# Second MLP, first pass two blocks at a time: the read of w_out words moved two groups ahead, sums in a new buffer, streamed pairs of w_in in four transfers

## The chip, the cores and the metric

The kernel runs on one core of one Trainium2 chip. The metric is device time in microseconds. One profiled execution of the kernel before lies beside three timed runs.

## The reference

Attention with a softmax over q's head dimension and over k's sequence, then two MLPs on the 4608 x 512 result, all float32. The part around the change is the second MLP's first product and its activation.

```python
def _moe2_ref(x, w_in, w_out):          # x 4608 x 512, w_in 512 x 2048, w_out 2048 x 512
    h = x @ w_in
    relu6 = np.clip(h + 3.0, 0.0, 6.0)
    g = h * relu6 / 6.0
    return (g @ w_out).astype(np.float32)
```

The weights come in as 64-bit floats, read as pairs of 32-bit words, and the kernel makes float32 of them by integer operations. Each float32 product is made of three matmuls with a high and a low part (`mm3`, L81 to L84).

## The kernel before

Each large product is done by a scheme of seven half-size products instead of eight: operands numbered 1 to 7 are sums and differences of quarters, and the results are added up from seven matmul chains. So a "pair" of w_in, which is 256 of its 2048 columns, is kept as 7 slices of 2 x 128 columns, each with a high and a low part. Such a pair is a tile of 128 x 3584 floats, 1792 KB, and lies ready in DRAM as `wd[1, p]`. There are 8 pairs (NC).

**The first pass of the second MLP** is the loop over `step_in(k)`, 40 steps (L978). Steps 0 to 7 are narrow: one block of 512 tokens, matmuls of 256 columns. Steps 8 to 39 are wide: two blocks at a time, matmuls of 512 columns, four rounds of eight steps (round 0 is steps 8 to 15). Each step uses one pair p = k mod 8 and has 7 products of 6 matmuls, 42 in all. TensorE's order within a step is: product 7 of step k-1, products 6, 2 and 3 of step k, then product 1 of step k+1 (`head`, L903), product 4 of step k-1, product 5 of step k+1 (`head_5`, L917). Behind product 1 stands a ScalarE copy of bank A into bank B (L915, "copy B<-A"), and product 6 needs it. Between the two lie products 4, 5 and 7.

**Streamed pairs.** The odd pairs stay in the core's memory. The even ones share the two buffers of `ring` and are read again each round: when product 4 of an even pair is done, `refill` (L1030) asks for the pair that is used four steps on, in one transfer of 1792 KB on SyncE's queue (`fill`, L291). That is two steps ahead of its first use, product 1 of `head`. Pair 7 is read in the same way after step 2.

**Gates and their stores.** ScalarE makes the relu of each result (L929), VectorE multiplies (L932) into tiles `gh` (two buffers), `gl` (three) and, in narrow steps, `g` (three), and SyncE's queue stores them to DRAM as `gd`: 256 KB for each `gh`, twice a step, 512 KB for `gl`. These transfers stand on the same queue as the pairs.

**Preparation of w_out.** Beside rounds 0 to 2 the kernel turns the second MLP's w_out into operands, pair by pair, and stores them. `weight_jobs` (L1043) writes the jobs of all 8 pairs out as a list of groups, 7 for each pair. `step_in` calls `slot(i)` three times a step (after product 6, after product 3, and at its end), and each call takes one group, but for the five slots in BUSY (L1057). The jobs of a pair, with the tile each uses:

| job | engine | work |
|---|---|---|
| feed | ScalarE's queue | transfer of the next pair's words, 1 MB, into `st` (one buffer) |
| mag | ScalarE | Abs of the words, `st` to `w` (L132); it waits until the words are there |
| floor, shift, sign, low | VectorE | integer operations on `w`; sign and low also read `st` |
| sum_0, sum_1 | GpSimd | four differences and sums of quarters of `w`, written into `st` itself (L196) |
| high_0, low_0, keep_0 | ScalarE, VectorE, ScalarE's queue | first 3 slices of the pair: high part, low part, store of 768 KB |
| high_1, low_1, keep_1 | the same | the other 4 slices, from the sums: high part (L212), low part (L216), store of 1 MB (L223) |

Because the sums lie in `st`, `feed` can be asked for only when low_1 has read them. Its group is the sixth of the seven, two groups ahead of the `mag` that needs the words.

All engines take their instructions in the program's order. The order is fixed by the code, so a waiting instruction holds back all behind it on its engine or queue.

Of the kernel before, what the change touches and what calls it, by code (L numbers as in the profile page):

```python
# [9 lines left out]
F32R = mybir.dt.float32r  # L10
# [7 lines left out]
P = 128  # L18
# [20 lines left out]
def attention_two_mlps(ctx: ExitStack, tc: tile.TileContext, kqT, kv5, qn, w1, w2, out):  # L39
    nc = tc.nc  # L40
# [28 lines left out]
    def f32(ap):  # L69
        return ap.bitcast(F32)  # L70
# [91 lines left out]
    wd = {}  # L162
# [19 lines left out]
    def operands_w(m, p, new_r, new_s, get_w, add=nc.vector):  # L182

        x = {}

        def sums(k):
            w = get_w()
            if k == 0:
                x["s"] = new_s()
            a22, a11, a12, a21 = (w[:, j * 256:(j + 1) * 256] for j in range(4))  # L190
            s1, s2, s3, s4 = (x["s"][:, j * 256:(j + 1) * 256] for j in range(4))
            for o, a, b, op in (
                (s1, a21, a22, ALU.add), (s2, s1, a11, ALU.subtract),
                (s3, a11, a21, ALU.subtract), (s4, a12, s2, ALU.subtract),
            )[2 * k:2 * k + 2]:
                add.tensor_tensor(out=o, in0=a, in1=b, op=op)  # L196

        def parts(k):
            src, n = ((get_w()[:, :768], 3), (x["s"], 4))[k]
            o = slice(0, 3) if k == 0 else slice(3, 7)  # L200
            src = src.rearrange("p (s n) -> p s n", n=256)
            if m == 2:
                return x["r", k][:, 0], x["r", k][:, 1], src
            return x["r"][:, 0, o], x["r"][:, 1, o], src

        def high(k):
            if m == 2:
                x["r", k] = m2_p[0].tile([P, 2, 3 + k, 2 * P], F32R, tag=f"r{k}", name="r")
            elif k == 0:
                x["r"] = new_r()  # L210
            h, l, src = parts(k)
            nc.scalar.copy(h, src)  # L212

        def low(k):
            h, l, src = parts(k)
            nc.vector.tensor_tensor(out=l, in0=src, in1=f32(h), op=ALU.subtract)  # L216

        def store_part(k):
            if (m, p) not in wd:
                wd[m, p] = dram.tile([P, 14 * 256], F32, tag=f"wd{m}{p}", name="wd")  # L220
            d = wd[m, p].rearrange("p (h s n) -> p h s n", h=2, n=256)
            o = slice(3 * k, 3 + 4 * k)
            nc.scalar.dma_start(out=d[:, :, o], in_=f32(x["r", k] if m == 2 else x["r"][:, :, o]))  # L223

        def keep():
            wd[m, p] = d = dram.tile([P, 14 * 256], F32, tag=f"wd{m}{p}", name="wd")
            nc.scalar.dma_start(out=d, in_=f32(x["r"]).rearrange("p h s n -> p (h s n)"))

        if m:
            keep_part = store_part if (m, p) != (1, STAYS) else lambda k: None  # L230
            return [
                (0.85, lambda: sums(0)), (0.85, lambda: sums(1)), (0, lambda: high(0)), (0.95, lambda: low(0)),
                (0, lambda: high(1)), (1.2, lambda: low(1)), (0, lambda: keep_part(0)), (0.5, lambda: keep_part(1)),
            ]
        return [
            (0.85, lambda: sums(0)), (0.85, lambda: sums(1)), (0, lambda: high(0)), (0.95, lambda: low(0)),
            (0.6, lambda: high(1)), (0.6, lambda: low(1)), (0.5, keep),
        ]
# [48 lines left out]
    def load_w(g):  # L287
        m, t, p = place(g)
        fill(ring_tile(g), m, p if g != PER + 1 else 2)

    def fill(r, m, p):  # L291
        nc.sync.dma_start(out=f32(r).rearrange("p h s n -> p (h s n)"), in_=wd[m, p])
# [737 lines left out]
    def refill(k):  # L1030
        p = k % NC
        if p % 2 == 0 and k + 4 < STEPS:
            n = (p + 4) % NC
            second_in[n] = r = ring_tile(2 * PER + k)
            fill(r, 1, n)
        if k == 2:
            fill(second_in[7], 1, 7)
        if k >= STEPS - NC and p in OUT_AFTER:
            load_out(OUT_AFTER.index(p))

    OUT_AFTER = (1, 3, 4, 5, 6, 7)

    def weight_jobs():  # L1043
        jobs, late = [], []
        for p in range(NC):
            c = [c[1] for c in second(p, 1, add=nc.gpsimd)]
            mag, floor, shift, sign, low, sum_0, sum_1, high_0, low_0, high_1, low_1, keep_0, keep_1 = c
            more = [feed] * (p < NC - 1)
            jobs += [
                late + [mag], [floor, shift], [sign], [low, sum_0, sum_1], [high_1], [low_1, keep_1, *more],  # L1050
                [high_0, low_0],
            ]
            late = [keep_0]
        return jobs + [late]

    weights_2 = []
    BUSY = {(0, 0), (6, 2), (7, 0), (7, 1), (7, 2)}  # L1057
# [1 line left out]
    def side_in(k):  # L1059
        b, p = divmod(k - NC, NC)  # L1060
        f = lambda i, *parts: [lambda part=part: form_wide(i, part) for part in parts]
        sm = lambda i: [lambda: sums_wide(i)]
        if b < 0:
            table = {
                (0, 2): [lambda: load_wide(0, 0)], (2, 2): sm(0), (3, 1): sm(1), (3, 2): sm(2), (4, 1): sm(3),
                (4, 2): f(1, 0), (5, 0): f(1, 1) + f(5, 0), (5, 2): f(5, 1), (6, 0): f(6, 0) + [feed],
                (6, 1): f(6, 1), (7, 1): f(2, 0), (7, 2): f(2, 1) + f(3, 0, 1),
            }
        else:
            table = {(0, 0): f(7, 0), (0, 1): f(7, 1), (0, 2): f(4, 0, 1)}  # L1070
            if b < WIDE - 1:
                table.update({
                    (1, 0): [lambda: load_wide(b + 1, 0)], (1, 1): [lambda: load_wide(b + 1, 1)],
                    (3, 0): sm(0), (3, 2): sm(1), (4, 1): sm(2), (5, 0): sm(3),
                    (6, 2): f(1, 0, 1) + f(5, 0), (7, 0): f(5, 1) + f(6, 0), (7, 1): f(6, 1) + f(2, 0),
                    (7, 2): f(2, 1) + f(3, 0, 1),
                })

        def slot(i):
            if 0 <= b < WIDE - 1 and (p, i) not in BUSY and weights_2:  # L1080
                for fn in weights_2.pop(0):
                    fn()
            for fn in table.get((p, i), ()):
                fn()
            if b == WIDE - 1:
                if (p, i) == (0, 0):
                    while weights_2:
                        for fn in weights_2.pop(0):
                            fn()
                    prep.close()  # L1090
                    out_p["a"] = stack("out_a", 1, early, side="right")
                    load_g(0)
                    load_g(1)
                for fn in ahead_of_out().get((p, i), ()):
                    fn()

        return slot
# [240 lines left out]
    with tc.manual_schedule():  # L1338
# [107 lines left out]
        head_5(0)  # L1446
        for k in range(STEPS):
            step_in(k, side_in(k))
        step_in(STEPS, lambda i: None)
        step_out(0, 2)  # L1450
        step_out(1)
# [64 lines left out]
```

## Time and profile before

| what | value |
|---|---|
| median of three runs | 1680.01 us (1678.97 to 1680.22) |
| profiled execution, its own time | 1683.46 us |
| span of the profile | 1681.7 us, mean granted TensorE clock 0.986 |
| TensorE busy | 1616.2 us, 96% of the span |
| VectorE, ScalarE, GpSimd busy | 1182.7, 758.4, 248.3 us |
| moved by DMA | 412 MB, 245 GB/s over the span |

TensorE is busy nearly all the time, so the page's 40 slices matter more than its sums: 39 of TensorE's busy digits are 8 or 9, and the few 8s show where it waited. Time comes back only where TensorE is idle, or where its clock is at the lower of its two levels.

### The profile page before, as it was taken

The numbers are of one execution on the slowest core, as the hardware profiler recorded it, in microseconds if no ns is written. First come the engines' busy times: TensorE is split into PE (matmuls) and PEld (weight loads), VectorE is DVE, ScalarE is ACT, GpSimd is POOL, SyncE is SP. The second block draws the span as 40 slices with busy tenths as digits, with TensorE's granted clock in tenths as the row PEclk, the third lists the DMA queues.
The fourth block names the chain that finished last, engine by engine and source line by source line (L and its number), as shares of the span: only waits on it lengthen the run. The fifth ranks groups of instructions, "written<-read, shape, count | busy, mean of one in ns | idle before, by whom it ended". The sixth has DMA issues, their size and how long they took to land. (4 is left out here: it accounts for less than half of the span.)

```text
span 1681.7 us, 25454 instructions
## 1 busy us (share of the span) xinstructions
PE 1616.2 (96%) x9768; PEld 1397.3 (83%) x9768; DVE 1182.7 (70%) x1834; ACT 758.4 (45%) x1291; POOL 248.3 (15%) x174
## 2 busy tenths in 40 slices
PE   6999999999999999999999899989899999999998
PEld 4455888989898888888889877767678999999998
DVE  5999677575656657567876476657565787777775
ACT  4454555454444545444544445435354343333332
POOL 2121332222122222200000113120400000000000
PEclk8999999999999999999999999989999999999999
DMA  8488768778787878558897877877788943333332
GB/s 281 150 306 302 263 212 290 246 260 265 234 279 232 302 241 277 203 223 329 317 378 288 313 280 256 318 276 271 266 301 288 376 149 126 126 126 126 126 127 75
DMA packets 87330, 412.16 MB, mean 245 GB/s; under 512 B 12840, under 2 KB 16936, under 8 KB 63528
## 3 DMA queue, kind: packets, MB, share of 16 engines
q1 hardware_dynamic: 75048, 351.02, 59.5%
q10 hardware_dynamic: 12160, 59.51, 9.4%
q8 instruction: 77, 1.26, 0.3%
q14 instruction: 45, 0.37, 0.1%
HBM read 311.43 MB, written 99.06 MB: 244 GB/s over the span
## 5 line engine op out<-in xcount | busy, mean ns | idle before, releaser
L1262 PE MATMUL M<-kout,f 128*128 128x256 f32 x2268 | 275.4, 282 | 0.5 <-DVE f L1168 0.5
L1262 PEld LDWEIGHTS M<-kout,f 128*128 128x128 f32 x2268 | 273.4, 189 | 0.9 <-DVE f L1168 0.7
L82 PE MATMUL y<-gs,woh 128*128 128x512 f32 x512 | 204.6, 400 | 0.0
L83 PE MATMUL y<-gs,woh 128*128 128x512 f32 x512 | 202.5, 395 | 0.0
L84 PE MATMUL y<-gs,wol 128*128 128x512 f32 x512 | 200.1, 391 | 0.0
L79 DVE TENSOR_TENSOR gs<-g,gs 128x512 fp32r<-128x512 f32 x128 | 111.9, 875 | 62.7 <-ACT gs L78 62.2
L1166 ACT CAST f<-gt 128x1024 fp32r<-128x1024 f32 x72 | 75.5, 1049 | 178.1 <-PE M L1262 97.0
L681 ACT ACTIVATE g<-A 128x512 f32<-128x512 f32 x72 | 43.1, 598 | 186.9 <-DVE A L841 171.6
L82 PE MATMUL B<-o,ring 128*128 128x256 f32 x408 | 118.3, 290 | 7.9 <-DVE B L846 4.6
L82 PE MATMUL A<-op,ring 128*128 128x256 f32 x408 | 115.9, 284 | 1.7 <-DMA ring<-wd 1.7
L78 ACT CAST gs<-g 128x512 fp32r<-128x512 f32 x128 | 79.2, 618 | 83.0 <-DVE g L683 80.0
L84 PE MATMUL B<-o,ring 128*128 128x256 f32 x408 | 115.5, 283 | 0.0
L83 PE MATMUL B<-o,ring 128*128 128x256 f32 x408 | 115.3, 283 | 0.0
L83 PE MATMUL A<-op,ring 128*128 128x256 f32 x408 | 115.2, 282 | 0.1
L84 PE MATMUL A<-op,ring 128*128 128x256 f32 x408 | 115.2, 282 | 0.0
L84 PEld LDWEIGHTS y<-gs,wol 128*128 128x128 f32 x512 | 96.5, 188 | 21.7
L1168 DVE TENSOR_TENSOR f<-gt,f 128x1024 fp32r<-128x1024 f32 x72 | 88.0, 1222 | 30.6 <-ACT f L1166 29.6
L82 PEld LDWEIGHTS y<-gs,woh 128*128 128x128 f32 x512 | 96.9, 189 | 12.7
L83 PEld LDWEIGHTS y<-gs,woh 128*128 128x128 f32 x512 | 97.2, 190 | 8.7
L82 PEld LDWEIGHTS B<-o,ring 128*128 128x128 f32 x408 | 77.4, 190 | 25.9 <-DVE B L846 8.9
L1262 PE MATMUL M<-ring,f 128*128 128x256 f32 x756 | 93.5, 282 | 0.4 <-DVE f L1168 0.4
L1262 PEld LDWEIGHTS M<-ring,f 128*128 128x128 f32 x756 | 91.6, 191 | 0.7 <-DVE f L1168 0.6
(336 smaller groups left out, 3792.9 us busy)
## 6 DMA issues: line engine op xcount, KB each, us to landing
ring<-wd SPq DMA_DIRECT2D x84, 1792.0 KB
gt<-gd SPq DMA_DIRECT2D x36, 1024.0 KB
st<-w_dram SPq DMA_DIRECT2D x16, 1024.0 KB
st<-w_dram ACTq DMA_DIRECT2D x16, 1024.0 KB
gd<-gh SPq DMA_DIRECT2D x64, 256.0 KB
gd<-gl SPq DMA_DIRECT2D x32, 512.0 KB
ev<-kv_dram SPq DMA_DIRECT2D x24, 640.0 KB
wd<-ring ACTq DMA_DIRECT2D x8, 1792.0 KB
```

The costliest lines, as they stand in the source:

```text
L78: nc.scalar.copy(hi, src)
L79: nc.vector.tensor_tensor(out=lo, in0=src, in1=f32(hi), op=ALU.subtract)
L82: nc.tensor.matmul(o, lhsT=wh, rhs=xh, start=start, stop=False, **kw)
L83: nc.tensor.matmul(o, lhsT=wh, rhs=xl, start=False, stop=False, **kw)
L84: nc.tensor.matmul(o, lhsT=wl, rhs=xh, start=False, stop=stop, **kw)
L681: nc.scalar.activation(out=a, in_=hb, func=AF.Tanh, scale=0.5)
L1166: nc.scalar.copy(o[0], src)
L1168: nc.vector.tensor_tensor(out=o[1], in0=src, in1=f32(o[0]), op=ALU.subtract)
L1262: nc.tensor.matmul(M[:, h * 2 * P:(h + 1) * 2 * P], lhsT=a, rhs=b, start=p == 0 and h == 0 and e == 0, stop=p == NC - 1 and e == 2, skip_g ...
```

## The change

Three parts, all in the second MLP's first pass.

1. The groups of `weight_jobs` are cut anew. `feed` moves from the sixth group to the fourth, directly behind `low`, so the read is asked for four groups ahead of the `mag` that needs it. high_0 and low_0 come before high_1 and low_1 and each stands in a group of its own; keep_0 comes one group behind low_0, high_1 three groups behind the sums, low_1 one group behind high_1, keep_1 one group behind low_1. A pair's last two groups are merged with the next pair's first two. The list has 58 groups, one more than before, for 57 slots: the last group, keep_1 of the last pair, is issued at the first slot of round 3.
2. The sums are written into the low half of the tile `r1` (tag "r1"), where low_1 later puts its result, and no longer into `st`.
3. A streamed pair is read in four transfers (high and low part, slices 0 to 3 and 4 to 6: 512, 384, 512, 384 KB). `refill` only notes them; each slot issues one (two in narrow steps). Pair 7 is asked for after step 3 instead of step 2.

```diff
         def sums(k):
             w = get_w()
-            if k == 0:
+            if k == 0 and m == 2:
+                x["r", 1] = m2_p[0].tile([P, 2, 4, 2 * P], F32R, tag="r1", name="r")
+                x["s"] = f32(x["r", 1][:, 1]).rearrange("p s n -> p (s n)")
+            elif k == 0:
                 x["s"] = new_s()
...
         def high(k):
-            if m == 2:
-                x["r", k] = m2_p[0].tile([P, 2, 3 + k, 2 * P], F32R, tag=f"r{k}", name="r")
+            if m == 2 and k == 0:
+                x["r", k] = m2_p[0].tile([P, 2, 3, 2 * P], F32R, tag="r0", name="r")
+            elif m == 2:
+                pass
...
+    pieces = []
+
+    def fill_in_pieces(r, p):
+        d = wd[1, p].rearrange("p (h s n) -> p h s n", h=2, n=2 * P)
+        for h in range(2):
+            for a, b in ((0, 4), (4, 7)):
+                pieces.append((f32(r[:, h, a:b]), d[:, h, a:b]))
+
+    def next_piece():
+        if pieces:
+            o, i = pieces.pop(0)
+            nc.sync.dma_start(out=o, in_=i)
...
         if p % 2 == 0 and k + 4 < STEPS:
             n = (p + 4) % NC
             second_in[n] = r = ring_tile(2 * PER + k)
-            fill(r, 1, n)
-        if k == 2:
-            fill(second_in[7], 1, 7)
+            fill_in_pieces(r, n)
+        if k == 3:
+            fill_in_pieces(second_in[7], 7)
...
             jobs += [
-                late + [mag], [floor, shift], [sign], [low, sum_0, sum_1], [high_1], [low_1, keep_1, *more],
-                [high_0, low_0],
+                late + [mag], last + [floor, shift], [sign], [low, *more, sum_0, sum_1], [high_0], [low_0],
+                [keep_0, high_1],
             ]
-            late = [keep_0]
-        return jobs + [late]
+            late, last = [low_1], [keep_1]
+        return jobs + [late, last]
...
             for fn in table.get((p, i), ()):
                 fn()
+            for _ in range(2 if b < 0 else 1):
+                next_piece()
...
         for k in range(STEPS):
             step_in(k, side_in(k))
+        while pieces:
+            next_piece()
```

How the instructions now stand, at three places. **ScalarE, round 1**, from the cast of a pair's second part (before) and from the read of the next pair's words (now) to the Abs that needs those words (L132) and the copy B<-A behind it. `st` is the tile of words, `d_8737` holds `w`, `r` the operands, `wd` their home in DRAM. Before:

```order
L915 COPY B_10089<-A_10088 128x512
L929 ACTIVATE gh<-A_10076,half 128x512
L926 COPY s_10112<-C_10105 128x512
L929 ACTIVATE gl<-B_9931,half 128x512
L223 DMA wd<-r 256x1x1024
L106 DMA st<-w_dram 128x2048
L929 ACTIVATE gh<-d_8737,half 128x512
L212 CAST r<-d_8737 128x768
L929 ACTIVATE gl<-A_10088,half 128x512
L223 DMA wd<-r 256x1x768
L132 ACTIVATE d_8737<-st 128x1024
L915 COPY B_10169<-A_10168 128x512
```

and now:

```order
L106 DMA st<-w_dram 128x2048
L947 ACTIVATE gl<-A_10038,half 128x512
L217 CAST r<-d_8737 128x768
L933 COPY B_10121<-A_10120 128x512
L947 ACTIVATE gh<-A_10107,half 128x512
L944 COPY s_10144<-C_10137 128x512
L947 ACTIVATE gl<-B_9956,half 128x512
L947 ACTIVATE gh<-d_8737,half 128x512
L228 DMA wd<-r 256x1x768
L217 CAST r<-r 128x1024
L947 ACTIVATE gl<-A_10120,half 128x512
L132 ACTIVATE d_8737<-st 128x1024
```

Between the read and its Abs stood three computing instructions; now there are nine, and no store of 1 MB stands directly ahead of the read.

**SyncE's queue, narrow steps.** `ring` and `k_8733` are pairs being read (`k_8733` is pair 7), `gd` the stores of gates. Before:

```order
L292 DMA ring<-wd 128x3584
L951 DMA gd_8871<-g_8806 128x1024
L951 DMA gd_8871<-g_8868 128x1024
L292 DMA ring<-wd 128x3584
L292 DMA k_8733<-wd 128x3584
L951 DMA gd_8998<-g_8929 128x1024
```

and now:

```order
L969 DMA gd_8870<-g_8806 128x1024
L307 DMA ring<-wd 128x1024
L307 DMA ring<-wd 128x768
L307 DMA ring<-wd 128x1024
L307 DMA ring<-wd 128x768
L969 DMA gd_8870<-g_8867 128x1024
L969 DMA gd_8999<-g_8932 128x1024
L307 DMA ring<-wd 128x1024
L307 DMA ring<-wd 128x768
L307 DMA ring<-wd 128x1024
L307 DMA ring<-wd 128x768
L969 DMA gd_8999<-g_8996 128x1024
```

A pair now stands behind the store of its step instead of ahead of it, and the two pairs that stood back to back are parted by a store.

**SyncE's queue, wide steps**, one streamed pair and the stores up to the next. Before:

```order
L292 DMA ring<-wd 128x3584
L973 DMA gd_9330<-gh 128x512
L975 DMA gd_9298<-gl 128x1024
L973 DMA gd_9330<-gh 128x512
L973 DMA gd_9492<-gh 128x512
L975 DMA gd_9298<-gl 128x1024
L973 DMA gd_9492<-gh 128x512
L292 DMA ring<-wd 128x3584
```

and now:

```order
L307 DMA ring<-wd 128x1024
L307 DMA ring<-wd 128x768
L991 DMA gd_9345<-gh 128x512
L307 DMA ring<-wd 128x1024
L991 DMA gd_9508<-gh 128x512
L993 DMA gd_9312<-gl 128x1024
L307 DMA ring<-wd 128x768
L991 DMA gd_9508<-gh 128x512 x2
L993 DMA gd_9475<-gl 128x1024
L307 DMA ring<-wd 128x1024
```

No store of a gate stands behind more than two pieces, and a pair's last piece is issued a step after its first.

## Rows read from the trace of the kernel before

**Rows 1.** Busy time by window; columns: window, length, engines' busy us (instructions), clock, DMA share, GB/s.

```profile
950.00:970.00 20.00, 15.71 (x80) 14.05 (x80) 11.71 (x18) 8.38 (x13) 0.00 (x0) 0.83 0.76 294
1010.00:1030.00 20.00, 16.03 (x59) 12.33 (x58) 11.67 (x17) 8.86 (x13) 11.35 (x7) 0.83 0.85 307
1090.00:1110.00 20.00, 12.09 (x42) 9.30 (x41) 10.48 (x15) 6.83 (x12) 0.00 (x0) 0.74 0.82 287
1190.00:1210.00 20.00, 16.03 (x60) 12.94 (x61) 12.15 (x18) 8.97 (x14) 5.12 (x2) 0.83 0.76 291
```

**Rows 2.** Who TensorE waited for, 930 to 1260 us; columns: total us, times, longest us.

```profile
PE B L82 <- ACT B L915: 19.7, 7, 7.9
PE B L82 <- DVE B L981: 3.5, 1, 3.5
PE A L83 <- DVE fw L594: 2.5, 4, 0.8
PE B L82 <- DVE d L981: 2.3, 2, 1.1
PE A L82 <- DMA ring<-wd: 1.7, 1, 1.7
PE A L82 <- DVE gh L932: 1.6, 1, 1.6
```

**Rows 3.** Timeline of TensorE; columns: start us, us, instruction, [idle before <- releaser].

```profile
934.01 0.39 PE L82 MATMUL A<-op,ring 128*128 128x256 f32 x1 [1.67 <-DMA ring<-wd]
953.52 0.58 PE L82 MATMUL B<-o,k 128*128 128x256 f32 x1 [3.49 <-DVE B L981]
...
1019.02 0.79 PE L82 MATMUL B<-e,k 128*128 128x512 f32 x1 [3.97 <-ACT B L915]
...
1101.00 0.79 PE L82 MATMUL B<-e,ring 128*128 128x512 f32 x1 [7.91 <-ACT B L915]
...
1193.97 0.80 PE L82 MATMUL B<-e,ring 128*128 128x512 f32 x1 [5.45 <-ACT B L915]
```

**Rows 4.** Timeline of ScalarE and its queue (ACTq) before the two longest waits.

```profile
1088.62 0.66 ACTq L106 DMA_DIRECT2D st<-w_dram  x1
...
1099.34 1.12 ACT L132 ACTIVATE d<-st 128x1024 f32<-128x1024 f32 x1 [7.92 <-DMA st<-w_dram]
...
1187.07 1.05 ACT L212 CAST r<-st 128x1024 fp32r<-128x1024 f32 x1 [2.30 <-POOL st L196]
...
1190.64 0.52 ACTq L223 DMA_DIRECT2D wd<-r  x1
1191.19 2.11 ACTq L106 DMA_DIRECT2D st<-w_dram  x1
1193.34 0.57 ACT L915 COPY B<-A 128x512 f32<-128x512 f32 x1 [4.64 <-issue]
```

**Rows 5.** Timeline of SyncE's queue in the narrow steps: two pairs asked for.

```profile
923.85 0.32 SPq L292 DMA_DIRECT2D ring<-wd  x1
...
936.09 0.43 SPq L292 DMA_DIRECT2D k<-wd  x1
```

**Rows 6.** Timeline of VectorE in the narrow steps: a gate waits for its buffer.

```profile
950.70 0.69 DVE L932 SCALAR_TENSOR_TENSOR g<-a,A 128x512 f32<-128x512 f32 x1 [5.45 <-DMA gd<-g]
```

**Rows 7.** Who ScalarE waited for, 930 to 1260 us: the relu of gh.

```profile
ACT gh L929 <- DMA gd<-gh: 21.7, 9, 4.9
```

**Rows 8.** Busy time by window, as rows 1: first MLP, narrow steps, round 1, round 3.

```profile
841.00:884.00 43.00, 42.78 (x266) 38.07 (x265) 33.02 (x52) 18.61 (x31) 2.39 (x1) 1.00 0.97 380
914.00:965.00 51.00, 45.84 (x347) 44.77 (x346) 22.06 (x41) 19.98 (x38) 7.17 (x3) 0.93 0.82 309
1048.00:1140.60 92.60, 81.86 (x338) 64.38 (x337) 61.02 (x79) 42.17 (x63) 16.56 (x12) 0.94 0.79 287
1216.00:1300.00 84.00, 83.86 (x362) 67.58 (x362) 54.49 (x78) 42.32 (x64) 0.00 (x0) 1.00 0.85 301
```

**Rows 9.** Groups by line, 914 to 1320 us: VectorE's job low (x8).

```profile
L150 DVE SCALAR_TENSOR_TENSOR d<-st,d 128x1024 uint32<-128x1024 uint32 x8 | 9.7, 1218 | 0.0
```

More of the change, by code (lines that the diff above doesn't have):

```diff
@@ L1043, in weight_jobs @@
     def weight_jobs():
-        jobs, late = [], []
+        jobs, late, last = [], [], []
         for p in range(NC):
```

## Prediction

> **What bounds the kernel now.** The first view is busy time by window. In round 3, from 1216 to 1300 us, TensorE works 83.86 of 84 us at the full clock [rows 8], 362 matmuls in all, so a wide step of 42 takes 42 x 84 / 362 = 9.75 us, and there is nothing to gain there. The windows of [rows 1] look different: TensorE is idle for 4 to 8 of their 20 us, and the granted clock is 0.74 to 0.83, a mixture of the full 2.4 GHz and of 1.2 GHz. All four lie between 950 and 1210 us, beside the narrow steps and rounds 0 to 2.
>
> The second view says whom TensorE waited for. Its six rows add up to 31.3 us, and 19.7 of them are waits of product 6 for ScalarE's copy of bank A into bank B [rows 2]. The timeline then gives each long gap its time: 3.49, 3.97, 7.91 and 5.45 us [rows 3], one in each of the four windows. So the clock fell beside the four gaps of 3.49 to 7.91 us, and not after that of 1.67. What the lower clock takes is (1 - clock) times 20 us: 3.4, 3.4, 5.2 and 3.4 us [rows 1], 15.4 us together. Gaps and clock make 31.3 + 15.4 = 46.7 us. That is all that this stretch can give back.
>
> The third view is the engine that TensorE waited for. At 1099 us ScalarE's Abs stood 7.92 us for the words of the next pair, 10.7 us after their read had been issued at 1088.62, and the copy stood behind it [rows 4]. At 1190 us it was a chain: the cast of the sums waited 2.30 us for GpSimd, VectorE's low part waited for that cast, and the store and the read, which stand ahead of the copy on ScalarE's queue, waited for VectorE, so the copy was 4.64 us late [rows 4]. The gap of 3.49 us has another root: VectorE waited 5.45 us for a gate buffer whose store had not landed [rows 6], because two pairs stood ahead of it on SyncE's queue.
>
> **The change part by part.**
>
> *The groups of the jobs.* A slot is 9.75 / 3 = 3.25 us. The read of words goes from two groups ahead of the Abs (6.5 us) to four (13 us). It took at most 10.7 us in the row above, and there a store of 1 MB stood directly ahead of it, so the Abs finds its words. The cast of the sums now comes three groups after them, and each low part and store a group behind what it needs, so the chain is gone too. I take off all waits for the copy, 19.7 us, and the clock of their three windows, 3.4 + 5.2 + 3.4 = 12.0: **minus 31.7 us**.
>
> What is new there: the read must wait until VectorE's `low` has read `st`, and this time it stands in the same group. `low` takes 1.22 us [rows 9]; with a gate's multiply ahead of it (0.69 us, as in [rows 6]) and 0.66 us to issue [rows 4], ScalarE is held up to 2.6 us. The copy behind it has products 4, 5 and 7 as cover, 18 matmuls of 9.75 / 42 us, 4.2 us, and takes 0.57. So it costs nothing; if ScalarE comes late to it, it costs about 1 us at each of the slots that stand just ahead of a copy, three of the seven, which the range holds. The sums on GpSimd now wait for the store of `r1`, issued two groups (6.5 us) before; they are wanted three groups later, 9.75 us, and GpSimd is otherwise idle: nothing.
>
> *Pieces, narrow steps.* The gaps of 1.67 and 3.49 us and the clock of their window, 3.4, are 8.6 us. The store of a gate now stands behind one pair at most, so the 3.49 should shrink. But these steps are short of transfers: 309 GB/s for 51 us is 15.8 MB [rows 8], and without the 8.6 us it would be 15.8 / 42.4 = 372 GB/s, as much as the fullest stretch of the trace, 380 GB/s. Pair 7 is asked for a step later than before (it was at 936.09 [rows 5]), and every pair behind a store. Bounds: all 8.6 us back, or 3 us worse, about one further gap like the 3.49. I take half: **minus 4.3 us**.
>
> *Pieces, wide steps.* The relu of gh waited 21.7 us in nine places for its buffer's store [rows 7]. ScalarE's waits show on TensorE as the rows "d" and "gh" of [rows 2], 2.3 + 1.6 = 3.9 us. With stores between pieces I take half back: **minus 2.0 us**. The 2.5 us for "fw" are the operands of the next two blocks; the change does not touch them, and they stay.
>
> The last piece of a pair is issued three slots after the first and used three slots, 9.75 us, after that. A whole pair of 1792 KB, issued at 923.85 [rows 5], was there at 934.01 [rows 3], 10.2 us, behind whatever stood ahead of it. A piece of 512 KB should take a third, so no piece is late: nothing, with the rival below for the other end.
>
> *New costs.* The last store of w_out falls into the first slot of round 3, and one of two loads for the second pass waits on SyncE's queue until it has landed, with stores and two pieces behind: **plus 1 us** (0 to 3.4). And rounds 0 to 2 get tighter. Round 1 moved 287 GB/s for 92.6 us, 26.6 MB [rows 8]; in 8 x 9.75 = 78 us that is 341 GB/s, nine tenths of 380. Short waits come back: **plus 3 us** (0 to 12).
>
> Sum: -31.7 - 4.3 - 2.0 + 1 + 3 = **-34.0 us**. The profiled execution took 1683.46 us (span 1681.7 and 1.8 around it) and would take 1649.5. The median of the runs is 1680.01, 3.4 us below it, so I predict **1646 us**.
>
> **The rivals.**
>
> *Transfers become the bound.* Round 3 ran at 301 GB/s with the DMA engines 0.85 busy and no wait [rows 8]. If rounds 0 to 2 can't move more than that, 26.6 MB take 88.4 us, and each of two rounds like round 1 gives 4 us, the narrow steps 4: about 1668 us. For it: the queues are 0.79 busy already and the pieces add 57 transfers. Against it: 380 GB/s for 43 us at 0.97 [rows 8], with loads and stores mixed. The Trainium skill, page "DMA: Bandwidth & Descriptors", section Specifications, puts the share of HBM of one core at about 358 GB/s. The first row of [rows 8] is above that, so the measurement decides; by the page 341 would be 95% of the limit, and this rival likelier than I make it.
>
> *The read is asked sooner and is late all the same*, because ScalarE gets to it late (it waits for VectorE) or one buffer of words is not free. Then the Abs keeps its long wait, 7.91 + 5.2 us, and the time is about 1659. Against it: the order shows nine instructions between them now, and the only readers of `st` left are sign and low.
>
> *Slower: the queue pays for every piece.* If SyncE's queue dealt with its transfers one after the other, each with a fixed cost, the five transfers of a step (three stores, two pieces) would not fit into 9.75 us, and TensorE would stand at product 1 or 6 of each streamed pair. There are 14 pairs whose load starts in a wide step. Late by 3.5 us each, without any loss of clock, they cost 49 us: 1695 us. It decides from 34 / 14 = 2.4 us on. Against it: round 3 already has 3.5 transfers a step with 2.0 MB, and SyncE's pairs left no gap in TensorE there. The Trainium skill has this cost, on the same page, section "Anatomy of one DMA": about 2.0 us for each and the bytes at 436 GB/s. One after the other, that would be an estimated 11.5 us for a step before and 14.5 us now, 28 x 4.75 = 133 us more than the 9.75. But round 3's step of 9.75 us is already less than 11.5 [rows 8], so by the trace the fixed part of one transfer passes beside others, and I give this little.
>
> *No change*: the waits move to another place of the same length. Half the 46.7 us would have to come back as new gaps and clock; I see no single place for it.
>
> **How the numbers follow.** The forecast has 0.62, the transfers 0.15, the late read 0.13, slower 0.07, no change 0.03. A difference of 0.2%, 3.4 us, is about what a measurement of this kernel can tell from none. Faster is 0.62 + 0.15 + 0.13 = 0.90, same 0.03, slower 0.07. The forecast's own range is 1638 (all of the 8.6 us back, nothing new) to 1655 (12 us of short waits). Eight in ten reach to the two rivals on the same side: 1638 to 1668.
>
> **What would show it.** The waits of TensorE for "ACT B" fall from 19.7 us to under 3; the Abs (L132) has no wait for `st`; the cast of `r` none for GpSimd; the clock is 1.00 in every 20 us window from 970 to the end of the pass; round 1 takes 78 to 82 us at 330 GB/s; what is left lies in the narrow steps, at "ring", "k" or "g". I am wrong if a new row of TensorE's waits names a DMA of `ring` in wide steps, if the clock still falls there, or if round 1 stays near 90 us.

## The result and the profile after

The changed kernel takes 1661.45 us, the median of four runs (1656.24 to 1667.13), against 1679.49 for the kernel before (1677.62 to 1680.22): a ratio of 0.9895, 95% interval 0.986 to 0.993. It is faster, by 18 us where 34 were forecast. The profiled execution of the changed kernel is the shortest of its four, 1656.24 us with a span of 1654.4 and a mean clock of 0.995.

First the question on which most of the forecast rested: whom does TensorE wait for now? The view of waits, 930 to 1260 us; columns as in [rows 2]:

```profile
PE A L84 <- DMA ring<-wd: 12.4, 6, 5.3
PE A L82 <- DMA ring<-wd: 1.0, 1, 1.0
PE A L84 <- DMA k<-wd: 0.8, 1, 0.8
PE A L83 <- DVE fw L612: 0.8, 1, 0.8
PE B L84 <- DMA ring<-wd: 0.3, 1, 0.3
```

The seven waits for ScalarE's copy, 19.7 us in [rows 2], have no row left. Those for VectorE's "B", "d" and "gh" are gone too. In their place stands a row that was not there: pieces of streamed pairs, 12.4 us in six waits, all at L84, the matmul that takes the low part. Busy time by window, the four windows of [rows 1] and then rounds 1 and 2:

```profile
950.00:970.00 20.00, 16.69 (x96) 13.98 (x95) 10.50 (x16) 9.80 (x15) 0.00 (x0) 1.00 0.74 277
1010.00:1030.00 20.00, 20.00 (x88) 16.20 (x87) 15.06 (x20) 10.54 (x17) 6.96 (x6) 1.00 0.96 353
1090.00:1110.00 20.00, 20.00 (x88) 16.19 (x87) 16.50 (x20) 11.12 (x17) 6.06 (x3) 1.00 0.87 316
1190.00:1210.00 20.00, 19.86 (x86) 15.79 (x85) 15.76 (x21) 12.98 (x19) 0.00 (x0) 1.00 0.72 251
...
1036.60:1116.40 79.80, 78.48 (x337) 62.97 (x336) 63.97 (x81) 43.49 (x64) 15.86 (x12) 1.00 0.89 319
1116.40:1196.50 80.10, 78.86 (x338) 62.83 (x338) 61.40 (x79) 43.45 (x64) 20.40 (x16) 1.00 0.85 305
```

The granted clock is 1.00 in all four windows where it was 0.74 to 0.83, and TensorE fills three of them. Round 1 takes 79.8 us, not 92.6 [rows 8], at 319 GB/s. Where the new waits lie, by the timeline of TensorE:

```profile
930.61 0.39 PE L84 MATMUL A<-op,ring 128*128 128x256 f32 x1 [1.49 <-DMA ring<-wd]
942.98 0.39 PE L84 MATMUL A<-op,ring 128*128 128x256 f32 x1 [2.15 <-DMA ring<-wd]
949.05 0.38 PE L84 MATMUL A<-op,k 128*128 128x256 f32 x1 [0.80 <-DMA k<-wd]
955.06 0.50 PE L82 MATMUL A<-fw,ring 128*128 128x512 f32 x1 [1.02 <-DMA ring<-wd]
957.28 0.50 PE L84 MATMUL A<-fw,ring 128*128 128x512 f32 x1 [1.49 <-DMA ring<-wd]
...
1075.05 0.51 PE L84 MATMUL A<-fw,ring 128*128 128x512 f32 x1 [1.18 <-DMA ring<-wd]
...
1154.57 0.50 PE L84 MATMUL A<-fw,ring 128*128 128x512 f32 x1 [0.82 <-DMA ring<-wd]
...
1219.53 0.80 PE L84 MATMUL A<-fw,ring 128*128 128x512 f32 x1 [5.27 <-DMA ring<-wd]
```

Five lie in the stretch that is called narrow below (the last two at product 1 of step 8, the first wide one). Three more, of 1.18, 0.82 and 0.28 us, lie in rounds 1 and 2. The longest, 5.27 us, is at the start of round 3, where the kernel before had no wait. What stands behind it is read from ScalarE's queue (ACTq), from SyncE's, and from the waits of SyncE's queue:

```profile
1202.96 0.52 ACTq L228 DMA_DIRECT2D wd<-r  x1
...
1201.79 0.44 SPq L1149 DMA_DIRECT2D gt<-gd  x1
1211.70 0.32 SPq L1149 DMA_DIRECT2D gt<-gd  x1
1212.11 0.38 SPq L991 DMA_DIRECT2D gd<-gh  x1
1212.55 0.42 SPq L307 DMA_DIRECT2D ring<-wd  x1
...
1214.75 0.43 SPq L307 DMA_DIRECT2D ring<-wd  x1
```

```profile
SPq L1149 <- DMA wd<-r: 9.4, 1, 9.4
```

At 1202.96 ScalarE's queue issues the last store of w_out, the 58th group. SyncE's queue stands before the second load for the second pass (L1149) until 1211.70, and the view of waits gives that row 9.4 us, "DMA wd<-r". Behind it stand the stores of gates and the last two pieces of a pair, its low part, at 1212.55 and 1214.75. TensorE wants the first of the two at 1214.26 (1219.53 less 5.27) and goes on at 1219.53. The clock pays too; the window behind the gap:

```profile
1220.00:1224.00 4.00, 4.00 (x11) 3.03 (x11) 1.31 (x3) 1.18 (x2) 0.00 (x0) 0.50 0.57 220
```

**Stage by stage.** The first matmul of product 5 marks each step in TensorE's timeline. From step 3's to step 8's is called "narrow" here, from 8's to 16's round 0, then rounds 1 and 2, and from 32's to 37's the start of round 3. An undisturbed round is 78 us (8 x 9.75), the start of round 3 is 49.2. One profiled execution each, us; medians and ratios (to the kernel before on the same chip, 95%) are of the timed runs:

| kernel | narrow | round 0 | round 1 | round 2 | start of 3 | median | ratio |
|---|---|---|---|---|---|---|---|
| before | 33.99 | 85.32 | 92.57 | 91.71 | 49.16 | 1679.49 | 1 |
| changed | 33.82 | 77.61 | 79.80 | 80.05 | 57.36 | 1661.45 | 0.9895 (0.986 to 0.993) |
| changed, again | 37.93 | 78.91 | 79.53 | 79.69 | 56.80 | 1660.69 | 0.9897 (0.988 to 0.9913) |
| whole pairs | 34.70 | 78.97 | 79.78 | 80.45 | 51.45 | 1653.15 | 0.9856 (0.9837 to 0.9875) |
| pieces alone | 34.51 | 84.69 | 91.09 | 88.06 | 49.24 | 1679.1 | 1.001 (0.9993 to 1.0027) |
| store early | 34.29 | 77.60 | 79.33 | 79.67 | 49.16 | 1649.35 | 0.984 (0.9824 to 0.9856) |
| store early, whole pairs | 32.48 | 78.73 | 80.34 | 80.45 | 49.16 | 1651.78 | 0.9839 (0.9821 to 0.9858) |
| store early, whole in narrow | 34.25 | 77.85 | 79.84 | 80.22 | 49.17 | 1648.56 | 0.9827 (0.98 to 0.9853) |
| pair 7 sooner | 36.10 | 79.85 | 79.33 | 79.29 | 49.21 | 1647.69 | 0.9816 (0.9796 to 0.9837) |
| read late | 35.09 | 79.61 | 79.97 | 84.90 | 49.16 | 1654.09 | 0.9853 (0.9831 to 0.9876) |
| old grouping | 36.55 | 79.76 | 80.64 | 83.38 | 49.18 | 1657.12 | 0.986 (0.9838 to 0.9883) |
| pair 7 first | 39.14 | 78.93 | 79.46 | 80.43 | 49.22 | 1657.19 | 0.9857 (0.9835 to 0.988) |
| high pieces at once | 31.77 | 78.02 | 79.78 | 79.41 | 49.19 | 1645.63 | 0.9801 (0.9784 to 0.9819) |
| four pieces at once | 32.49 | 77.98 | 80.23 | 80.27 | 49.19 | 1648.39 | 0.9818 (0.9801 to 0.9834) |

From "store early" on, every row has the last store of w_out within round 2 ("old grouping" by its own list).

### The profile page after: what moved, and what is told of

It reads as the page before. It is cut to its first block, busy times and chain, and to the rows that moved or that the text cites. A ratio compares the mean times of both kernels' runs of the same rounds, so it can differ in the third digit from the quotient of the medians.

```text
span 1654.4 us, 25538 instructions
## 1 busy us (share of the span) xinstructions
PE 1603.8 (97%) x9768; PEld 1389.2 (84%) x9768; DVE 1191.4 (72%) x1834; ACT 758.5 (46%) x1291; POOL 247.3 (15%) x174
## 4 chain that ended last, share of the span: by engine, by line
PE 66%; DVE 8%; DMA 7%; ACT 2%; issue 2%; SPq 0%; ACTq 0%; DVEq 0%
PE M L1282 19%; PE y L82 6%; PE y L83 5%; PE y L84 5%; PE A L84 4%; PE B L82 4%; PE A L83 4%; PE B L84 4%; PE A L82 4%; PE B L83 4%; DMA ring<-wd 4%; DMA gd<-gh 2%; DMA gt<-gd 2%; PE C L84 1%; PE C L83 1%
## 5 line engine op out<-in xcount | busy, mean ns | idle before, releaser
L84 PE MATMUL y<-gs,wol 128*128 128x512 f32 x512 | 200.2, 391 | 0.0
L84 PE MATMUL A<-op,ring 128*128 128x256 f32 x408 | 115.4, 283 | 3.6 <-DMA ring<-wd 3.6
L84 PE MATMUL B<-o,ring 128*128 128x256 f32 x408 | 115.2, 282 | 0.0
L84 PEld LDWEIGHTS y<-gs,wol 128*128 128x128 f32 x512 | 96.4, 188 | 21.7
```

What stands on the lines that cost most here:

```text
L84: nc.tensor.matmul(o, lhsT=wl, rhs=xh, start=False, stop=stop, **kw)
```

## The experiments

### The changed kernel again

No edit.

> The changed kernel once more, for its spread and a second profile. It ran between 1656 and 1667 us where the kernel before stays within 3 us. Theory A (two places are marginal: a streamed pair is waited for in the narrow steps and at the start of round 3, and each gap sometimes brings the lower clock with it): median 1656 to 1667, and the profile has its gaps at just these two places, 12 to 22 us in all, rounds 0 to 2 within 2 us of 8 x 9.75 = 78 each. Theory B (rounds 0 to 2 are at the limit of transfers and run differently each time): gaps in the wide steps of rounds 0 to 2 too, a round of over 82 us.

It measured 1660.69 us in five runs (1658.26 to 1666.96), so the 1661 us hold. The rounds and the start of round 3 agree with the first profile within 1.3 us; the narrow steps do not, 37.93 against 33.82. Busy time by window, 908 to 965 us, first of the changed kernel, then of this run:

```profile
908.00:965.00 57.00, 49.25 (x369) 46.18 (x368) 26.74 (x47) 22.71 (x41) 7.16 (x3) 1.00 0.79 293
```

```profile
908.00:965.00 57.00, 50.06 (x351) 47.77 (x350) 24.46 (x45) 19.78 (x38) 7.17 (x3) 0.90 0.78 290
```

TensorE is busy longer and does less: 351 matmuls against 369, at a clock of 0.90 against 1.00. The gaps differ by less than 1 us each (1.49, 2.15, 0.80, 1.02 and 1.49 above; 1.77, 1.85, none at pair 7, 1.86 and 1.46 here), and the clock falls in one execution and not in the other.

### Which part does it: the groups with whole pairs, the pieces alone

"Whole pairs": the changed kernel with streamed pairs read in one transfer, pair 7 after step 2.

```diff
-            fill_in_pieces(r, n)
-        if k == 3:
-            fill_in_pieces(second_in[7], 7)
+            fill(r, 1, n)
+        if k == 2:
+            fill(second_in[7], 1, 7)
```

> The new groups and the new home of the sums, with whole pairs in one transfer, as before. Theory A (the groups carry the gain, 32 us by the prediction's term, the last store costs 7.5 us of it, the pieces give next to nothing): 1650 to 1660 us, no wait of TensorE for the copy B<-A. Theory B (the pieces carry a good part, because stores of gates stood behind whole pairs): 1665 us or more, with waits for gate buffers back in rounds 1 and 2.

"Pieces alone": the kernel before with the pieces, their functions and their calls in the slots, and nothing else of the change.

```diff
-            fill(r, 1, n)
-        if k == 2:
-            fill(second_in[7], 1, 7)
+            fill_in_pieces(r, n)
+        if k == 3:
+            fill_in_pieces(second_in[7], 7)
```

> The pieces alone, with the groups and the sums' home of the kernel before. Theory A: the four long waits for the copy stay, 1675 to 1685 us, no change to be measured or a little slower in the narrow steps. Theory B: 1660 to 1670 us.

TensorE's waits, 930 to 1260 us, of the pieces alone and then of the whole pairs with the new groups:

```profile
PE B L82 <- ACT B L928: 12.9, 6, 5.7
PE A L84 <- DMA ring<-wd: 9.6, 7, 2.1
```

```profile
PE B L82 <- DVE B L999: 3.8, 1, 3.8
PE B L82 <- DVE d L999: 3.1, 3, 1.1
PE B L82 <- ACT B L933: 2.0, 1, 2.0
```

The pieces alone leave the waits for the copy (L928 is its line there), add waits for pieces, and change the time by nothing that twelve runs can tell: 1.001 (0.9993 to 1.0027). The groups and the sums' home (the two were not parted) do all of it: with whole pairs the kernel is faster than the change as made, 1653.15 us. So the change's own pieces cost it 7.5 us (1660.69 less 1653.15), and the table says where: the start of round 3 is 51.45 us with whole pairs and 57.36 with pieces. SyncE's queue waits for the last store as long (11.3 us there), but a whole pair had been asked for at 1198.30, ahead of the wait; with pieces two of its four stood behind it. What the late store still costs with whole pairs, 51.45 against 49.16 us, is one wait of TensorE for the copy, 2.04 us: the copy stands behind a relu that waits 9.14 us for its gate's buffer.

### The last store a group sooner

```diff
-        return jobs + [late, last]
+        return jobs + [late + last]
```

> The changed kernel with the last store of w_out in the last group of round 2, one group earlier than the first slot of round 3, so that there are 57 groups. Theory A (SyncE's queue stood 9.4 us because a load for the second pass waited for this store, and the pair's third piece behind it came late): the wait of SyncE's queue for the store is gone, the gap of 5.3 us at the third piece in round 3 and the low clock behind it too, 7.5 us less than the changed kernel, about 1654. Theory B (two loads of 1 MB ahead of the pieces are what makes them late): the gap stays at 3 us or more, and the time within 3 us of the changed kernel.

> New groups and sums' home, the last store in round 2, whole pairs in one transfer: against the run with the last store early it takes away the pieces alone. Theory A (with the store out of the way the pieces neither cost nor bring anything): within 2.5 us of that run, 1647 to 1652. Theory B (pieces let stores of gates through in wide steps): 1652 us or more, with TensorE waits for gates in rounds 0 and 1. Theory C (each piece costs something on the queue): 1646 or less.

The second is the same with whole pairs. "Store early" measured 1649.35 us (1647.51 to 1654.74), 11 less than the changed kernel on the same chip. SyncE's queue has no wait for "wd<-r" any more, and the start of round 3 is 49.16 us as in the kernel before. That place is 7.6 to 8.2 of the 11 us. The other 3 can't be placed: the narrow steps, whose code is the same in both, take 34.29 us here and took 33.82 and 37.93 in the two profiles of the changed kernel. Its waits of TensorE:

```profile
PE A L84 <- DMA ring<-wd: 5.4, 5, 1.7
PE A L84 <- DMA k<-wd: 2.4, 1, 2.4
PE A L83 <- DVE fw L612: 0.8, 1, 0.8
```

With whole pairs it is 1651.78, ratios 0.9839 and 0.984: once the store is out of the way, the pieces are neither a gain nor a loss that these runs can tell. They do what the prediction took them for at the gates, though. The relu's wait for its buffer, 930 to 1260 us, with the store early in both, first with whole pairs and then with pieces, and last with the pieces alone in the old groups:

```profile
ACT gh L947 <- DMA gd<-gh: 45.9, 17, 6.6
```

```profile
ACT gh L947 <- DMA gd<-gh: 23.9, 10, 4.5
```

```profile
ACT gh L942 <- DMA gd<-gh: 9.9, 5, 3.9
```

In the old groups the pieces bring the 21.7 us of [rows 7] down to 9.9. In the new groups the shorter rounds double it with whole pairs; with pieces it stays about where it was. But with whole pairs and the store early TensorE loses only 2.7 us to "d", so there is little to win.

### Which of the two causes: the read's place or the chain

The new groups do two things: the read of words is asked for sooner and no longer behind a store of 1 MB, and the casts and stores no longer form a chain ahead of the copy. "Read late" moves the read alone, to two groups ahead of its Abs as before; "old grouping" restores the order of casts and stores alone, with the read still behind `low`. Both also have the last store within round 2.

```diff
-                [sign], [low, *more, sum_0, sum_1], [high_0], [low_0],
+                [sign], [low, sum_0, sum_1], [high_0], [low_0, *more],
```

> The run with the last store early, but the words are asked for two groups ahead of the Abs again (in the group of low_0); the home of the sums and all else stay. It tells how much of the gain is the sooner asking. Theory A (two roots of similar size: the late words 14 us, the chain of sums 17 us): 1658 to 1665, the Abs waits again and TensorE for the copy behind it. Theory B (the chain was the root, the words came late because ScalarE asked late): within 4 us of that run, 1647 to 1654.

```diff
-                late + [mag], last + [floor, shift], [sign], [low, *more, sum_0, sum_1], [high_0], [low_0],
-                [keep_0, high_1],
+                late + [mag], [floor, shift], [sign], [low, *more, sum_0, sum_1], [high_1], [low_1, keep_1],
+                [high_0, low_0],
             ]
-            late, last = [low_1], [keep_1]
-        return jobs + [late, last]
+            late = [keep_0]
+        return jobs + [late]
```

> The changed kernel with the grouping of the jobs put back: Abs, magnitude, floor and shift, sign, low (with the sums of rows behind it), high_1, low_1 and keep_1, high_0 and low_0 in groups of their own in the order of the kernel before, keep_0 held over to the next round; pieces, the sums' own tile and the feed behind low stay as changed. To be set beside 1649.35 us, the same kernel with the short grouping and keep_1 stored at its round's end. Theory A, the long waits for copy B came from the chain of casts and stores that stood on ScalarE's queue ahead of the copy: PE's waits for copy B are back with 5 us or more in each of several steps, time 1657 to 1667. Theory B, it was the read of the next words that waited behind the store, and its leaving that place was enough: no wait for copy B over 2 us, time 1647 to 1654.

By the profiles both lie between. Rounds 0 to 2 together are 269.6 us before, 263.8 with pieces alone, 236.6 with the store early, 244.5 with the read late and 243.8 with the old grouping: either repair by itself brings 19 to 20 of the 27 us that both bring beyond the pieces. The timed runs leave less between them. The profile of the read late is its longest run, 1657.98 us, and that of the store early its shortest, 1647.51; the ratios of the single repairs, 0.9853 and 0.986, can't be told from the 0.984 of both. So each repair alone takes most of the loss away, and the long waits need both causes; whether the second adds 7 us or next to nothing stays open.

The read late, at 1654.09 us, lies at the upper edge of its theory B (1654); of theory A only the Abs's wait comes back, without a wait of TensorE for the copy. Neither theory on the old grouping holds: the waits for the copy do not come back, as its theory A had it, and the time is 3 us above the range of theory B. In that kernel, the waits of TensorE, one of ScalarE's, and the two longest gaps of round 2:

```profile
PE A L84 <- DMA ring<-wd: 10.1, 7, 2.2
PE B L82 <- ACT B L933: 1.4, 2, 1.1
...
ACT r L217 <- POOL r L199: 12.2, 7, 3.4
...
1162.11 0.50 PE L84 MATMUL A<-fw,ring 128*128 128x512 f32 x1 [2.19 <-DMA ring<-wd]
1168.57 0.49 PE L82 MATMUL B<-e,ring 128*128 128x512 f32 x1 [1.09 <-ACT B L933]
```

The cast waits for GpSimd again, 12.2 us in seven places, and the copy is late by 1.1 us at most; what it costs beyond that shows at the pieces. With the read late, ScalarE's Abs waits for its words again, and TensorE's loss too is at pieces (9.1 us):

```profile
ACT d L132 <- DMA st<-w_dram: 7.5, 3, 4.1
```

Its long round is round 2, 84.90 us, with two such gaps close together, 1.11 and 2.06 us, and a clock of 0.66 from 1160 to 1170 us.

### The narrow steps: bytes or order

Three kernels, and two more below, all with the store early. "Whole in narrow" reads the pairs that start in steps 0 to 7 in one transfer; "pair 7 sooner" asks for its pieces after step 1; "pair 7 first" reads it whole at the start of the pass.

```diff
-            fill_in_pieces(r, n)
-        if k == 3:
-            fill_in_pieces(second_in[7], 7)
+            if k < NC:
+                fill(r, 1, n)
+            else:
+                fill_in_pieces(r, n)
+        if k == 2:
+            fill(second_in[7], 1, 7)
```

> Last store early, pieces in the wide steps alone, whole pairs in the narrow steps and pair 7 after step 2, as before the change. Theory A (narrow steps are short of transfers whatever the order): within 2.5 us of the run with the last store early, 1647 to 1652, some 8 us lost in narrow steps. Theory B (the later asking of the pairs is what TensorE waits for there): 3 us or more faster, 1646 or less.

```diff
-        if k == 3:
+        if k == 1:
             fill_in_pieces(second_in[7], 7)
```

> The run with the last store early, but pair 7 is asked for after step 1 instead of step 3, where the transfers had pauses (about 144 to 250 GB/s between 922 and 938 us). Theory A (all that the narrow steps need is more than 380 GB/s can bring): no more than 1.5 us gained. Theory B (the order of asking leaves pauses): the waits for pairs 6, 7 and 0 fall by 3 to 6 us and the clock stays up, 1643 to 1647.

```diff
-        if k == 3:
-            fill_in_pieces(second_in[7], 7)
...
         fill(second_in[5], 1, 5)
+        fill(second_in[7], 1, 7)
```

> The version with keep_1 stored in a group of its own at the end of its round (measured at 1649.35 us), with pair 7 read whole at the start of the pass, beside pair 5, and no longer in the narrow steps. Theory A, the narrow steps are limited by the bytes of their whole stretch: the reads that follow come later by as much and the gap moves to the pairs read from pair 4 on; waits on pieces and on the k pair in the narrow steps stay at 7 to 10 us, time 1646 to 1651. Theory B, the transfers have slack at the start of the pass (138 to 233 GB/s there before) that can take the 1 MB: the waits in the narrow steps fall by 3 to 6 us, time 1641 to 1645.

The first two can't be told from "store early" (0.9827 and 0.9816 against 0.984), and the narrow steps are no shorter, 34.25 and 36.10 us against 34.29. With whole pairs in them the old waits are back, 1.66 us at pair 4 and 3.69 at VectorE's "B". With pair 7 asked for sooner its own wait is gone (2.4 us with the store early), and two at the ring are longer, 2.19 and 2.07 us. Pair 7 first is a miss for both its theories: 1657.19 us. SyncE's queue in it, and TensorE behind:

```profile
913.11 1.39 SPq L310 DMA_DIRECT2D k<-wd  x2
914.55 1.03 SPq L579 DMA_DIRECT2D xa<-yd  x1
923.91 0.32 SPq L969 DMA_DIRECT2D gd<-g  x1
924.33 0.85 SPq L307 DMA_DIRECT2D ring<-wd  x2
...
934.16 0.58 PE L82 MATMUL A<-op,ring 128*128 128x256 f32 x1 [4.25 <-DMA ring<-wd]
936.36 0.58 PE L84 MATMUL A<-op,ring 128*128 128x256 f32 x1 [1.41 <-DMA ring<-wd]
```

The gap has moved to pair 4, as theory A had it, but it is larger and the time 6 us above that theory's range. Pair 7's 1792 KB now stand ahead of pair 4 on the queue; pair 4 is asked for at 924.33, wanted at 929.91 and there at 934.16. So the start of the pass had no slack for them, and theory B falls. The rows show something else as well. Behind the transfer of 914.55 the queue issues nothing until 923.91: it stands before a gate's store (L969) that waits for VectorE, and pair 4's pieces stand behind that store. In the kernel before the whole pair went out ahead of it. Hence the last two runs: in the narrow steps the first two pieces, or for pair 4 all four, are issued where `refill` asks for them.

```diff
             fill_in_pieces(r, n)
+            for _ in range(2 if k < NC else 0):
+                next_piece()
```

> The version with keep_1 stored at its round's end (measured at 1649.35 us), with the two high pieces of a streamed pair issued at once in the narrow steps, ahead of the gate's store that waits for VectorE on the same queue (in that version the four pieces of pair 4 went out at 923.6 us behind such a store, where the kernel before sent the whole pair ahead of it, 3.7 us after its input load of the step). Theory A, this place behind the store is what makes the narrow steps late: product 1 finds its high part sooner, the waits for pieces and the k pair (4.1 us in three places there, and 1.7) fall by 2 us or more, time 1643 to 1647. Theory B, the bytes of the narrow steps are the limit: the waits move to other pieces or to gate buffers, time 1647 to 1651.

```diff
             fill_in_pieces(r, n)
+            for _ in range(4 if k == 0 else 2 if k < NC else 0):
+                next_piece()
```

> The same with all four pieces of pair 4 issued at once, as nothing waits for a gate buffer that early, and the two high ones of pair 6. Theory A: the wait of 1.7 us at pair 4 goes wholly and the steps behind it keep their times, 1642 to 1646. Theory B, the bytes of the narrow steps are the limit: the wait of 1.7 us stays or moves, time 1647 to 1651.

SyncE's queue, first with the store early, then with the high pieces at once:

```profile
923.15 0.32 SPq L969 DMA_DIRECT2D gd<-g  x1
923.56 2.20 SPq L307 DMA_DIRECT2D ring<-wd  x4
```

```profile
919.13 1.29 SPq L307 DMA_DIRECT2D ring<-wd  x2
...
921.62 0.32 SPq L969 DMA_DIRECT2D gd<-g  x1
921.99 1.41 SPq L307 DMA_DIRECT2D ring<-wd  x2
```

Counted from product 5 of step 0 (911.87 and 910.34 us), the first pieces leave after 8.8 us instead of 11.7, and the gate's store after 11.3 in both. In the kernel before the pair left after 8.8 too (923.85 [rows 5], step 0 at 915.06). The waits of TensorE from 930 to 1260 us become:

```profile
PE A L84 <- DMA k<-wd: 2.4, 1, 2.4
PE A L84 <- DMA ring<-wd: 1.9, 2, 1.2
PE A L83 <- DVE fw L612: 0.8, 1, 0.8
```

In the narrow steps no wait for `ring` is left (3.7 us with the store early), and they take 31.77 us, 2.5 less. The kernel takes 1645.63 us, ratio 0.9801 (0.9784 to 0.9819), and its interval lies below that of "store early" (0.9824 to 0.9856): theory A, the order and not the bytes. The same stretch of 905 to 960 us moves 325 GB/s in it, and 313 with the store early. The 2.4 us at pair 7 stay; a kernel that also asks for that pair sooner was not run. All four at once do not add to that. Theory A of that run wanted pair 4's wait gone, and 0.55 us of it stays; 1648.39 us lies in the range of its theory B (1647 to 1651) and can't be told from either neighbour. High pieces at once is the fastest of all kernels here, 34 us below the one before.

## Why the prediction was right, and where its size failed

The sum against the profiled execution of before, term by term, from the stages of the table (again is the run whose profile is its own median):

| term | predicted | changed | again |
|---|---|---|---|
| rounds 0 to 2: groups -31.7, gates -2.0, tighter +3 | -30.7 | -32.1 | -31.5 |
| narrow steps | -4.3 | -0.2 | +3.9 |
| last store of w_out | +1 | +8.2 | +7.6 |
| the rest (the profiled execution of before was long by 3.4) | -3.4 | -3.1 | -2.9 |
| sum, against 1683.46 | -37.4 | -27.2 | -22.8 |

**Right: what bounded the rounds, and what the groups would give back.** The waits for the copy and the low clock beside them went as forecast: rounds 0 to 2 are 31.5 to 32.1 us shorter, for 30.7, and 30.4 with whole pairs, so it is the groups that do it. The Abs finds its words, and `low` ahead of the read does hold ScalarE up as described, longer than I had it (3.8 us at most, for 2.6) and hidden all the same: the row "ACT B L933 <- DVE d L150" has 6.1 us in two waits, and TensorE none for the copy.

**Right in the direction, too small: the gates.** I took half of 3.9 us off for stores between pieces. All 3.9 went, and the 2.5 for "fw", which I had left standing, fell to 0.8 (as it did with whole pairs and with the pieces alone). With whole pairs "d" stays, at 3.1 us, so that part is the pieces' doing. The relu's wait fell by more than half with the pieces alone, 21.7 to 9.9 us; in the changed kernel, with its shorter rounds, the pieces only kept it from doubling.

**Wrong: "plus 1 us" for the last store.** The step itself was seen: a load waits on SyncE's queue for the store, "with stores and two pieces behind". Its price was not taken from the order. The store was issued at 1202.96 and the load let go at 1211.70, 8.7 us later; the low part was wanted at 1214.26. "No piece is late" fell here: I gave a piece of 512 KB a third of 10.2 us, and this one, issued at 1212.55, took until 1219.53, 7.0 us. By the third, 3.4 us, it would still have come 1.7 us late. That is the 5.27 us gap, and the clock with it: 7.6 to 8.2 us, over twice the upper end of 3.4. One line's edit gives it back.

**Wrong: "minus 4.3 us" for the narrow steps.** I reasoned from back-to-back pairs and from bytes. The rows of the order, quoted ahead of the prediction, showed the pair moving from ahead of the gate's store to behind it, and that store waits for VectorE; the prediction names this ("every pair behind a store") and puts no price of its own on it. It eats what the parted pairs give: the old waits of 1.67 and 3.49 us [rows 3] went, and five of 0.80 to 2.15 came. High pieces ahead of that store give 2.5 us back. Of the bounds, 8.6 us back or 3 worse, one execution lies inside (-0.2) and one just outside (+3.9).

**The signs.** Of the prediction's signs of being wrong two came, neither at the old place. TensorE waits for `ring` in wide steps, 1.18, 0.82, 0.28 and 5.27 us, and the clock falls once behind the last of them, to 0.50 in 1220 to 1224 us. The third, a round 1 near 90 us, did not come.

**The rivals.** Transfers were not the bound: round 1 ran at 319 GB/s with a clock of 1.00 where that rival had 301. The read was not late: no wait of L132 is left in the rounds, and that its 1659 us is near the time is chance, since the mechanism did not occur. The queue does not pay for every piece: 14 pairs, 42 more transfers in the wide steps, and the ratio of the pieces alone is 1.001, the upper end of its interval 1.0027 or 4.5 us, where that rival had 49 (its 3.5 us for a pair came from no row). The changed kernel's round 1 has five transfers on this queue in a step of 9.98 us (79.80 / 8). The Trainium skill, page "DMA: Bandwidth & Descriptors", section "Anatomy of one DMA", gives a transfer about 2.0 us of its own, for the path of transfers that GpSimd issues; these are issued by SyncE. If that figure held here, the prediction's estimate of 14.5 us for five in a row would not fit into 9.98, so that part would pass beside other transfers.

The forecast's own range of 1638 to 1655 did not hold the time, by 6 us. The wider range held it, but only by the part that was there for the transfers and the late read, and neither happened: that is luck. The forecast's 1646 is near what the kernel gives once the two queue orders are mended (1645.63), by terms that differ: by the profile the rounds gave 32.4 us, the narrow steps 2.2, and the last store cost nothing.

## What to carry to other kernels

Price a transfer by what its queue does before it: list the instructions ahead, and for each that waits on an engine or on another transfer read when that ends; a wait at the head of a queue delays every transfer behind it, however small the pieces. In this kernel pieces paid only when the first-used ones were issued where the buffer comes free, ahead of such a wait (0.9801, and 0.9839 with whole pairs). When two causes hide each other, mending either may bring most of the gain, and only undoing them one at a time shows it.

## What the runs showed of the hardware

A transfer that waits holds up all that stands behind it on its queue, and the price was larger than I had thought. Between 1201.79 and 1211.70 us SyncE issued nothing for 9.4 us, for one store of 1 MB on another queue, and 7.6 to 8.2 us of the kernel's time hung on it. The Trainium skill, page "DMA: Bandwidth & Descriptors", section "Anatomy of one DMA", says that such a wait happens on the sequencer that issues, before dispatch; the rows agree.

The same program, at the same place, kept the clock at 1.00 in one execution and had 0.90 in another, with gaps that differ by less than 1 us; that is 4.1 us in the narrow steps alone (33.82 and 37.93). In the profiled execution of the kernel before the clock fell beside gaps of 3.49 us and more and stayed up behind one of 1.67; in the second profile of the changed kernel it fell to 0.85 and 0.73 (930 to 934 and 934 to 938 us) beside one of 1.77. What decides it is left open. Five runs of one such kernel spread by 7 to 10 us (changed again, store early, whole in narrow, read late, old grouping), and a single profile of a stretch with gaps is no measure of an edit worth 2 us.
